# Three queries projected ahead of the first keys, part of the clearing on VectorE, and new stage priorities in a two-layer attention and MLP kernel

## The chip, the cores and the metric

The kernel runs on one core of a Trainium2 chip. The metric is the device time of one execution in microseconds (us). Every kernel below gave the right result. The engines are TensorE (PE in the profile, PEld for its weight loads), VectorE (DVE), ScalarE (ACT), GpSimd (POOL) and SyncE (SP, which here only issues transfers). L803 is line 803 of that kernel's own source, so one operation has different line numbers in different kernels.

## The reference

Two layers of sliding-window attention and MLP over 2048 tokens of 576 elements, in bfloat16; 32 heads of 18 elements, a window of 256.

```
x = x + A(layernorm(x), wqkv, wo)
x = x + B(layernorm(x), w1, b1, w2, b2)
x = x + A(layernorm(x), wqkv, wo)
x = x + B(layernorm(x), w1, b1, w2, b2)

A: q, k, v = x @ wqkv;  s = q k^T / sqrt(18), masked to 0 <= i - j < 256
   softmax(s) @ v @ wo
B: gelu(x @ w1 + b1) @ w2 + b2        # 576 -> 4608 -> 576
```

## The kernel before

The tokens are 16 tiles of 128. They go through each layer in four chunks of four tiles, and the attention of one chunk is laid beside the MLP and the projections of others, so that TensorE always has something to run.

The kernel holds its own list scheduler. Each operation is added with an estimated duration and a priority; the scheduler makes one fixed order for each engine. On the chip each engine then runs its list in that order, and waits where an input is not there.

```python
# the pick: earliest possible start first, then priority
for e in ENGS:
    for t in released[e]:
        st = max(free[e], t.ready)
        ...
        key = (round(st, 3), t.prio, t.idx)
        ...
# emission: the planned order, engine by engine
order = sorted(order + extra, key=lambda x: x[0])
for st, t in order:
    ...
        self.S.add(t.eng, t.fn, names(t.reads), names(t.writes), dma=t.dma, ring=t.ring)
return max(t.end for t in self.tasks)
```

A stage of the program has a name (`q1.0` is the projection of chunk 1, tile 0; `ma`, `mb`, `ga`, `gb` are halves of the MLP; `ea`, `eb` halves of attention; `t` the output projection), and `PL.nudge` adds a number to the priority of all its operations. These numbers were found by annealing. Up to the planned time `FEED_UNTIL` the scheduler also puts back a choice for TensorE that would let ScalarE run dry.

Statistics of a tile, its norm and the casts of queries are on VectorE; the norm is written to one of four buffers `xn`, and SyncE transposes it from there:

```python
add("dve", lambda e, i=i, s=s: e.bn_stats(st_all[:, t, i, :], s[:, t, i * HB:(i + 1) * HB]),
    reads=res, writes=[f"st{t}_{i}"], cost=0.37, lat=0.14, prio=prio)
...
sl = xn_ctr[0] % NXN                                   # NXN = 4
add("dve", lambda e: e.tensor_scalar(xn[:, sl, 0:D], s[:, t, :], mv_all[:, t, 0:1], rstd[:, t:t + 1],
                                      op0=ALU.subtract, op1=ALU.mult),
    reads=res + [f"mv{t}", f"rstd{t}"], writes=[f"xn{sl}"], cost=0.67 if src is None else 0.45, lat=0.14, prio=prio)
...
xin_load(4, 4, ["xa3"], -6)     # input tiles 4 to 7, held back until the first chunk's last transpose
...
xin_load(8, 4, ["k3"], -4)      # input tiles 8 to 11, held back until the fourth key
```

The names in the last two calls are gates only: the loads don't read `xa3` or `k3`, they are held back until these exist. Names in the profiles: `hT` at the start holds the loaded input, `mv_all` and `rstd` its statistics, `xnTa` and `xnTm` are the transposed norms that attention and MLP read, `qn` a cast query, `qT` its transpose, `pT` the exponentials of the scores, `attq` a scaled attention output, `attT` its transpose, `x_res` the residual, and `ps` a bank of PSUM, the memory that matmuls write.

The softmax here doesn't subtract the row's maximum and nothing guards it: scores larger than these inputs give would overflow.

## Time and profile before

| | kernel before |
|---|---|
| time at the outset, 3 runs | 927.13 us (924.19 to 928.40) |
| span of the profiled run | 924.9 us |
| TensorE busy | 900.4 us |
| TensorE idle | 24.5 us |
| VectorE busy | 320.2 us (35%) |
| time lost to TensorE's half clock between 8 and 905 us | 1.71 us, one stretch |

The last row sums 1 minus the granted clock over windows of 1 us (0.36 + 0.50 + 0.50 + 0.35 from 33 to 37 us). The lower clock in the last 0.9 us of the kernel before (0.59, behind its last matmul) is left out.

The prediction shows the busy times, the windows and the timeline. One more view lists what TensorE waited for: the operation that waited, the engine and operation that let it go, us in total, how many times, the longest. The lines of the kernel before with the most time on VectorE, GpSimd and one transfer:

```profile
PE ps L802 <- POOL pT L785: 4.2, 9, 1.0
...
PE ps L669 <- DMA xnTa<-xn: 1.5, 3, 0.8
...
PE ps L669 <- DVE qn L708: 1.1, 4, 0.4
PE ps L919 <- DVE x_res L836: 0.9, 4, 0.3
PE ps L802 <- DVE attq L817: 0.8, 2, 0.5
```

Waits for GpSimd's mask (pT, L785) lead.

A caution: this trace has 9374 matmuls where it has 9411 weight loads. So 37 matmul records are missing, and the idle time is overstated.

### The profile page before, as it was taken

How to read it: one execution, taken by the hardware profiler on the slowest of the kernel's cores; microseconds unless marked ns; L12 is line 12 of the kernel's file. 1: busy time of each engine (PE TensorE's matmuls, PEld its weight loads, DVE VectorE, ACT ScalarE, POOL GpSimd, SP SyncE). 2: the span in 40 equal slices, each digit the busy share in tenths (PEclk: the TensorE clock that was granted, in tenths of full speed). 3: DMA queues.
4: the chain of work that ended last, by engine and by line, in shares of the span. 5: the costliest groups of instructions: out<-in, count | busy, mean ns of one | idle time of the engine just before them, and what ended most of it. 6: DMA issues, size and time to landing. Idle time of an engine off the chain costs nothing.

```text
span 924.9 us, 22416 instructions
## 1 busy us (share of the span) xinstructions
PE 900.4 (97%) x9374; PEld 566.6 (61%) x9411; DVE 320.2 (35%) x796; ACT 598.2 (65%) x721; POOL 373.7 (40%) x507
## 2 busy tenths in 40 slices
PE   9898999999999999999999999999999999999998
PEld 6556475665756657475665657657575665656556
DVE  5647122642217332182324513352111620241001
ACT  4886686676757777566655767557687577852541
POOL 3877453462515535054331644316452363610100
PEclk9999999999999999999999999999999999999999
DMA  8996729743186333944367351693519626174430
GB/s 196 139 242 127 219 57 241 173 145 116 25 211 175 128 105 47 265 98 154 101 99 239 51 188 43 99 264 90 175 40 233 133 69 204 42 202 146 156 116 27
DMA packets 221460, 129.01 MB, mean 139 GB/s; under 512 B 151856, under 2 KB 219184, under 8 KB 221360
## 3 DMA queue, kind: packets, MB, share of 16 engines
q1 hardware_dynamic: 212048, 119.90, 52.3%
q0 software_dynamic: 6880, 5.03, 3.1%
q10 hardware_dynamic: 2432, 2.65, 0.9%
q8 instruction: 74, 1.21, 0.6%
q14 instruction: 26, 0.21, 0.1%
HBM read 91.87 MB, written 2.36 MB: 102 GB/s over the span
## 4 chain that ended last, share of the span: by engine, by line
PE 70%; DMA 3%; issue 2%; DVE 2%; POOL 2%; ACT 1%; POOLq 0%
PE ps L919 25%; PE ps L890 21%; PE ps L669 11%; PE ps L802 6%; PE ps L755 4%; PE ps L878 3%; DMA xnTm<-xn 2%; POOL pT L785 1%; ACT pT L764 1%; DMA xnTa<-xn 1%; DVE xn L613 1%; DVE x_res L836 1%; POOL x_res L901 0%; DVE st_all L590 0%; DVE xn L618 0%
## 5 line engine op out<-in xcount | busy, mean ns | idle before, releaser
L764 ACT ACTIVATE pT<-ps 128x1024 bf16<-128x1024 f32 (+2 forms) x384 | 348.2, 972 | 126.4 <-PE ps L755 125.4
L785 POOL TENSOR_SCALAR_AFFINE_SELECT pT<-pT 128x512 bf16<-128x512 bf16 (+1 forms) x368 | 282.1, 790 | 261.9 <-ACT pT L764 256.2
L919 PE MATMUL ps<-w_sb,hT 128*128 128x288 bf16 x2304 | 314.9, 286 | 1.8 <-DVE x_res L836 0.9
L893 ACT ACTIVATE hT<-ps,b1col 128x512 bf16<-128x512 f32 x288 | 198.0, 687 | 169.3 <-PE ps L890 169.3
L890 PE MATMUL ps<-xnTm,w_sb 128*128 128x512 bf16 x1115 | 255.1, 379 | 3.5 <-issue 2.4
L919 PEld LDWEIGHTS ps<-w_sb,hT 128*128 128x128 bf16 x2304 | 211.4, 97 | 74.0 <-issue 18.5
L890 PEld LDWEIGHTS ps<-xnTm,w_sb 128*128 128x128 bf16 x1152 | 108.9, 98 | 137.5 <-issue 17.4
L836 DVE TENSOR_TENSOR x_res<-ps,x_res 128x288 f32<-128x288 f32 x160 | 71.4, 450 | 257.0 <-PE ps L919 215.0
L669 PE MATMUL ps<-wqkv,xnTa 128*128 128x288 bf16 x960 | 135.8, 288 | 3.9 <-DMA xnTa<-xn 1.5
L802 PEld LDWEIGHTS ps<-vA,pT 128*128 128x128 bf16 x2880 | 94.0, 96 | 28.2 <-POOL pT L785 13.2
L669 PEld LDWEIGHTS ps<-wqkv,xnTa 128*128 128x128 bf16 x960 | 87.0, 98 | 36.4 <-issue 5.8
L802 PE MATMUL ps<-vA,pT 128*128 128x20 bf16 x2880 | 100.2, 171 | 5.3 <-POOL pT L785 4.2
L708 DVE CAST qn<-ps 128x288 bf16<-128x288 f32 x120 | 54.4, 455 | 111.6 <-PE ps L669 108.3
L901 POOL TENSOR_TENSOR x_res<-x_res,b2bc 128x576 f32<-128x576 f32 x32 | 44.9, 1402 | 93.9 <-ACT hT L893 93.9
L755 PE MATMUL ps<-qT,kT 32*128 32x384 bf16 (+2 forms) x1216 | 64.2, 277 | 2.9 <-ACT pT L764 1.9
L601 POOL TENSOR_SCALAR vtmp<-mv_all 128x1 f32<-128x1 f32 (+1 forms) x43 | 8.9, 206 | 131.2 <-DVE mv_all L592 129.8
L695 DVE CAST vA<-ps 128x288 bf16<-128x288 f32 x64 | 29.1, 456 | 54.8 <-PE ps L669 54.7
L590 DVE BATCH_NORM_STATS2 st_all<-x_res 128x6 f32<-128x288 f32 x104 | 44.8, 446 | 3.8 <-DMA x_res<-in_A_x_dram 2.4
L669 PE MATMUL ps<-wo_sb,attT 128*128 128x288 bf16 x320 | 45.0, 286 | 0.2 <-DVE x_res L836 0.2
L812 DVE RECIPROCAL rinv<-ps 128x16 f32<-128x16 f32 x64 | 16.3, 255 | 79.5 <-PE ps L802 79.2
L613 DVE TENSOR_SCALAR xn<-x_res,mv_all,rstd 128x576 bf16<-128x576 f32 x52 | 36.7, 709 | 14.8 <-DMA xnTm<-xn 9.6
L878 PE MATMUL ps<-xnTm,w_sb 64*128 64x512 bf16 x288 | 39.5, 377 | 1.2
(42 smaller groups left out, 279.7 us busy)
## 6 DMA issues: line engine op xcount, KB each, us to landing
w_sb<-in_B_w_dram SPq DMA_DIRECT2D x48, 864.0 KB, 6.3
w_sb<-in_B_w_dram SPq DMA_DIRECT2D x48, 768.0 KB, 4.8
w_sb<-in_B_w_dram SPq DMA_DIRECT2D x96, 48.0 KB, 4.5
x_res<-in_A_x_dram POOLq DMA_DIRECT2D x4, 1152.0 KB, 6.9
out_dram<-xn SPq DMA_DIRECT2D x16, 144.0 KB, 1.8
wqkv<-in_A_wqkv_dram ACTq DMA_DIRECT2D x3, 576.0 KB, 7.5
hT<-in_A_x_dram SPq DMA_DIRECT2D x2, 576.0 KB, 5.0
wo_sb<-in_A_wo_dram ACTq DMA_DIRECT2D x1, 576.0 KB, 6.2
```

The costliest lines, as they stand in the source:

```text
L613: add("dve", lambda e: e.tensor_scalar(xn[:, sl, 0:D], s[:, t, :], mv_all[:, t, 0:1], rstd[:, t:t + 1], op0=ALU.subtract, op1=ALU.mult), r ...
L669: ins = e.matmul(bank(bs[o])[:, 0:HB], lhs(c), rhs(c, o * HB), start=(c == 0), stop=(c == KD - 1))
L708: add("dve", lambda e, b=bs[o], dst=dst: e.tensor_copy(dst, bank(b)[:, 0:HB].rearrange("p (h d) -> p h d", d=DH)), reads=[bs[o]], writes=[ ...
L755: ins = e.matmul(two(bs[j // 2])[:, j % 2, col:col + nq * 128], k_of(T0 + so)[0][32 * j:32 * j + 32, g, :], qs[32 * j:32 * j + 32, g, qo * ...
L764: add("act", lambda e, h2=h2: e.activation(pT[:, sl, 2 * h2:2 * h2 + 2, lo:hi], two(bs[h2])[:, :, lo:hi], ACT.Exp, scale=SCALE), reads=[bs ...
L785: add("pool", lambda e, ap=ap, pat=pat, sgn=sgn, kind=kind: e.affine_select(ap, ap, pattern=pat, compare_op=(ALU.is_ge if kind == "d" else ...
L802: ins = e.matmul(bank(B_O)[:, o:o + VW], pT[:, sl, j, col + qi * 128:col + (qi + 1) * 128], vA[:, (T0 + so) % VS, 4 * g + j, :], start=(fi ...
L836: add("dve", lambda e: e.tensor_tensor(x_res[:, t, sl], bank(b)[:, 0:HB], x_res[:, t, sl], ALU.add), reads=[b], writes=[f"x{t}h{hh}"], cos ...
L878: ins = e.matmul(bank(bk)[:, 0:n], w1_sb[64 * b:64 * b + 64, sl, col:col + 128], xnTm[64 * b:64 * b + 64, k % 2, 4, 0:n], start=True, stop ...
L890: ins = e.matmul(bank(bk)[:, 0:n], w1_sb[:, sl, col:col + 128], xnTm[:, k % 2, c, 0:n], start=False, stop=(c == 3))
L893: add("act", lambda e, ff=ff, fl=fl, bk=bk: e.activation(hT[:, fl, 0:n], bank(bk)[:, 0:n], ACT.Gelu_apprx_tanh, bias=b1col[:, ff:ff + 1]), ...
L919: ins = e.matmul(bank(b)[:, 0:HB], hT[:, fl, i * 128:(i + 1) * 128], w2_sb[:, fl, hh * HB:(hh + 1) * HB], start=(fl == 0), stop=(fl == NFH ...
```

## The change

The intent: the first chunk's queries need a slow transposing transfer (a median 3.3 us to land in the kernel before) and its first keys don't, so three queries go first; GpSimd's clearing at the start is shared with VectorE; the stage priorities are annealed anew for the changed program.

```diff
-FEED_UNTIL = 75.0
+FEED_UNTIL = 40.0
...
-    PL.nudge = {"": 0.63, "ld0+": 7.4, "q1.0": -16.88, "q1.1": 0.39, ...       # 44 numbers, cut
+    PL.nudge = {"": -2.02, "q1.0": -2.58, "q1.1": 0.31, "ln2": 19.43, ...      # 49 numbers, cut
...
-        add("pool", lambda e, i=i: e.memset(qn[:, i, :]..., 0.0), ...)
+        add("dve" if i % 3 == 1 else "pool", lambda e, i=i: e.memset(qn[:, i, :]..., 0.0), ...)
-    add("pool", lambda e: e.memset(attq[:, :, D:KD * 128], 0.0), writes=["aqd"], cost=0.5, prio=-8)
+    add("dve", lambda e: e.memset(attq[:, :, D:KD * 128], 0.0), writes=["aqd"], cost=0.25, prio=-8)
...
-    QK0 = {("q", 0): -5.0, ("k", 0): -4.9, ("q", 1): -4.8, ("q", 2): -4.7, ("k", 1): -4.6, ("q", 3): -4.5, ...}
+    QK0 = {("q", 0): -5.0, ("q", 1): -4.9, ("q", 2): -4.8, ("k", 0): -4.7, ("q", 3): -4.6, ("k", 1): -4.5, ...}
```

## The prediction

> **What bounds the kernel now.** I read the page's busy times first, then windows of 100 us, then the timeline between 24 and 40 us. The busy times:
>
> ```profile
> span 924.9 us, 22416 instructions
> ...
> PE 900.4 (97%) x9374; PEld 566.6 (61%) x9411; DVE 320.2 (35%) x796; ACT 598.2 (65%) x721; POOL 373.7 (40%) x507
> ```
>
> TensorE is busy for 900.4 of 924.9 us, so 24.5 us of it are idle in view. No other engine is above 65%. The list of operations by engine shows that the change removes no matmul of the model: 2304, 1440, 960+320, 2880 and 1408 stay, and only dummy matmuls on the tile `warm` go from 47 to 44. A reordering can therefore win only what lies between matmuls. Where that is:
>
> ```profile
> core 0: us, PE busy (x) PEld busy (x) DVE busy (x) ACT busy (x) POOL busy (x), PEclk, DMA share, GB/s
> 0.00:100.00 100.00, 90.44 (x1189) 61.54 (x1191) 59.90 (x162) 71.55 (x92) 65.33 (x104) 0.98 0.94 170
> 100.00:200.00 100.00, 97.77 (x1064) 59.72 (x1070) 36.21 (x91) 71.59 (x84) 46.15 (x61) 1.00 0.67 163
> ...
> 800.00:925.00 125.00, 120.39 (x889) 74.56 (x892) 23.90 (x58) 52.61 (x69) 16.12 (x22) 1.00 0.43 127
> ```
>
> Idle is 100 - 90.44 = 9.56 us in the first 100 us, 10.3 us in the next 700 (24.5 - 9.56 - 4.61), and 4.6 us at the end. Of that last part 3.35 us follow the last matmul, which ends at 903.75 + 17.80 = 921.55; the order of TensorE after the last attention is the same in both kernels, so it stays. Of the first 9.56 us, 1.11 come before the first dummy and stay too.
>
> The first window also has a mean clock of 0.98. The timeline shows why, and this is the one large flaw that the change can reach:
>
> ```profile
> 28.95 0.79 PE L669 MATMUL ps<-wqkv,xnTa 128*128 128x288 bf16 x5
> 29.57 0.77 PE L802 MATMUL ps<-vA,pT 128*128 128x20 bf16 x24
> 30.88 0.40 PE L755 MATMUL ps<-qT,kT 32*128 32x384 bf16 x8 [0.54 <-DVE mv_all L592]
> 32.07 0.79 PE L669 MATMUL ps<-wqkv,xnTa 128*128 128x288 bf16 x5 [0.79 <-DMA xnTa<-xn]
> ...
> 33.41 1.38 PE L669 MATMUL ps<-wqkv,xnTa 128*128 128x288 bf16 x5
> 34.72 0.51 PE L755 MATMUL ps<-qT,kT 32*128 32x384 bf16 x4
> 35.35 1.38 PE L669 MATMUL ps<-wqkv,xnTa 128*128 128x288 bf16 x5
> ```
>
> At 32.07 the first projection of the second chunk waits for the transposed input. Two idle pieces, 0.54 and 0.79 us, stand together, and from about 33.4 five projections take 1.38 us where they took 0.79. In windows of 1 us the granted clock is 0.64, 0.50, 0.50 and 0.65 from 33 to 37, so 0.36 + 0.50 + 0.50 + 0.35 = 1.7 us of TensorE are lost to the clock. The flaw costs 0.54 + 0.79 + 1.7 = 3.0 us.
>
> Why the input is late is in the transfers:
>
> ```profile
> 24.56 0.37 SPq L534 DMA_DIRECT2D hT<-in_A_x_dram  x1
> 24.73 1.44 DVE L613 TENSOR_SCALAR xn<-hT,mv_all,rstd 128x576 bf16<-128x576 bf16 x4
> ...
> 25.18 6.46 SPq L633 DMA_TRANSPOSE xnTa<-xn  x4
> ...
> 25.63 2.00 POOL L962 DMA_DIRECT2D b1col<-in_B_b_dram  x1
> ```
>
> A load of 576 KB is issued on SyncE just ahead of the four transposes, and GpSimd's bias loads join them. The transposes then take a median 6.2 us to land; those of qT a little earlier took 3.3.
>
> [...] TensorE was 46% and 28% busy in the microseconds from 30 and 31. [...] in the changed program the VectorE clearings of qn have 32x7 elements against 32x14 on GpSimd. [...] no row here shows a clearing that slows GpSimd.
>
> **Part 1, clearing.** GpSimd loses two of six clearings of qn (six take 2.53 us, so 0.42 each) and attq (0.31): 2 x 0.42 + 0.31 = 1.15 us. Its last clearing would end at 4.31 - 1.15 = 3.16 instead of 4.31. But its next work starts at 4.57, after the first tile's statistics (VectorE, 4.27 + 0.21 = 4.48), so none of it is on the path. VectorE gains three. From warm (128 elements, 0.17) and wqkv (864, 0.78) one element costs about 0.83 ns, so 224 elements take 0.25 and 128 take 0.17: 2 x 0.25 + 0.17 = 0.67. It now ends its clearing at 2.22 + 0.30 = 2.52, so then at 3.19; the first tile is picked up at 3.42. Hidden by 0.2 us. Sum: 0.
>
> **Part 2, queries first.** TensorE executes 65 projections before the first scores in the old order and 70 in the new, 5 x 0.122 = 0.6 us more (0.122 us a matmul of 288 columns: the last 144 take 17.80, less a drain of 0.29, over 143). Against that, three queries are ready for their slow transposes about 1 to 2 us earlier, and the key, which needs only TensorE and a copy of 1.01 us, comes later. All of this is filled with projections that have to run anyway, so I count 0 on TensorE. What matters is the issue order on SyncE: in the new one the first transpose of the second chunk's input stands ahead of the 576 KB load, with the other three behind it. The TensorE work before the second chunk's first projection is otherwise the same (120 projections, 36 of the 20-column matmuls, the same scores), plus 3 dummies (0.33 us). I expect the wait at 32.07 to shrink below 0.3 us and the half clock to go: -3.0 + 0.3 = -2.7.
>
> **Part 3, priorities.** Counted as runs of one kind of matmul, the old order has 771 and the new 757. At full rate I get 3584 x 0.1224 + 1152 x 0.216 + 48 groups of edge matmuls x 0.65 + 2880 x 0.026 + some 41 for scores + 8 for transposes and dummies = 843 us. The rest of the busy time, 900.4 - 843 - 1.7 = 56 us, is drain and restart: 56/771 = 0.073 us a run. Fourteen fewer are -1.0 (an estimate from these rows). In the old order two waits for the mask, 0.90 at 81.09 and 0.99 at 84.21, follow long runs of the output projection; in the new one these are spread and 30 more input projections run before the first MLP matmul. I credit half, -0.9. Against this, between the last output projection and the first MLP matmul there now stand 50 input projections, 80 of the small ones and four score groups: 50 x 0.122 + 80 x 0.026 + 4 x 0.3 = 9.4 us, where it was 96.67 - 77.67 = 19.0. In that time the residual, statistics, rstd and norm (about 0.9 + 0.8 + 0.2 + 0.8 + 1.0 = 3.7) and a transpose (3.3 to 6.2) must finish: 7 to 10 us. Two dummies stand just before that MLP matmul, so the scheduler itself left a gap there. I charge +1.0. For the 10.3 us of small idles from 100 to 800, nearly all in pieces under 0.5 us, I expect a net -0.8. Sum: -1.0 - 0.9 + 1.0 - 0.8 = -1.7.
>
> Total: 927.1 - 2.7 - 1.7 = 922.7; I say 922.5.
>
> **Rivals.** (a) The wait moves instead of going. The transposed tile is still caught behind the bias column, whose tiny packets fill the queues (median 9.7 us to land), and the half clock stays: then only part 3, 925 to 927. For it: DMA share is 4.5 and 2.0 in the two microseconds from 30. Against: the tile's transpose now has no large load ahead. (b) The tight path into the first MLP stage becomes a wait of 2 to 3 us that costs the clock a window of 1.7 more: 926 to 929. For it: the arithmetic above and the two dummies. (c) ScalarE is the bound in the first chunk's attention (9.59 of 10 us busy from 60 to 70), so nothing there gets shorter. Against: TensorE holds other work, and its idle in 40 to 80 is only 2.95 us. (d) The new priorities remove half of the idle in 100 to 800 too: 916 to 918.
>
> **Range and chances.** Two per cent is 18.5 us. All idle that this change can touch is 24.5 - 3.35 - 1.11 = 20.0 us with 1.7 for the clock, so faster by 2% would need nearly all of it: 0.02. Slower by 2% would need several clock windows lost and new waits in most stages: 0.01. The old times spread over 4.2 us by themselves. Range 914.5 to 928.5.
>
> **What would show it.** Right: the granted clock is 1.00 from 30 to 40 us, the first 100 us show TensorE busy for about 93, no wait over 0.3 us for xnTa near 32, and the first clearing-dependent work on GpSimd still starts at 4.5. Wrong: a low clock anywhere in 25 to 110 us, a wait of over 1 us for xnTm before the first MLP matmul, or TensorE idle from 100 to 800 us above 13 us or below 6.

## The result, and the profile after

| | before | after |
|---|---|---|
| time, median (lowest to highest), 4 runs each | 926.65 us (924.19 to 928.40) | 934.72 us (934.08 to 935.38) |
| ratio to before, 95% interval | | 1.0089 (1.0064 to 1.0114) |
| span of the profiled run | 924.9 us | 932.9 us |
| TensorE busy / idle | 900.4 / 24.5 us | 900.9 / 32.0 us |
| idle, 100 to 800 us | 10.4 us | 15.2 us |
| lost to half clock | 1.71 us, one stretch | 3.42 us, two stretches |

A ratio is the mean time of one kernel's fast runs over that of the other's in the same rounds, so it isn't quite the ratio of the medians. The change made the kernel 0.9% slower. That is outside my range, and on the other side of the time before.

The page of the kernel after, its span and busy times, and two of its windows of 100 us (columns as in the prediction):

```profile
span 932.9 us, 22409 instructions
...
PE 900.9 (97%) x9372; PEld 566.1 (61%) x9408; DVE 319.9 (34%) x799; ACT 598.4 (64%) x721; POOL 372.0 (40%) x504
```

```profile
0.00:100.00 100.00, 87.98 (x1162) 61.17 (x1163) 64.53 (x167) 67.99 (x88) 61.85 (x98) 0.98 0.92 172
100.00:200.00 100.00, 94.54 (x1017) 56.40 (x1021) 31.19 (x83) 71.66 (x85) 45.02 (x60) 0.98 0.66 157
```

TensorE's busy time grew by 0.5 us only; 7.5 of the 8.0 us are idle time. The first two windows hold most of it: 90.44 - 87.98 = 2.5 us and 97.77 - 94.54 = 3.2 us. The clock of the second window is now below 1 too.

What TensorE waited for in the kernel after, the lines that answer to those of before:

```profile
PE ps L670 <- DVE qn L709: 3.1, 5, 1.5
PE ps L920 <- DVE x_res L837: 3.1, 6, 1.6
PE ps L670 <- DVE x_res L837: 2.5, 2, 1.6
PE ps L803 <- DVE attq L818: 2.5, 3, 1.6
...
PE ps L803 <- POOL pT L786: 2.1, 5, 0.9
```

This is most of the difference in one view. Waits for VectorE are 3.1 + 3.1 + 2.5 + 2.5 and two smaller of 0.6 and 0.5: 12.3 us in place of 4.1. Waits for the mask halved, and those for xnTa are gone. Waits for ScalarE rose too, from 2.7 us to 6.3, with one of 1.89 at 149.85; the last experiment on this kernel, all_moves_3, comes level with the kernel before while they stay at 6.5. Yet VectorE is busy for 34% of the span, as before. So it is not short of time; what TensorE needs from it stands in its queue behind something else. The timeline shows behind what, for the first of the large waits (columns: start, us, engine, line, operation, tiles; in brackets the idle time before it and who ended it):

```profile
26.36 1.42 SPq L535 DMA_DIRECT2D hT<-in_A_x_dram  x1
...
32.20 0.82 DVE L591 BATCH_NORM_STATS2 st_all<-hT 128x6 f32<-128x288 bf16 x2 [1.66 <-DMA hT<-in_A_x_dram]
...
33.22 0.46 DVE L818 TENSOR_TENSOR attq<-ps,rinv 128x288 bf16<-128x288 f32 x1
...
33.82 0.45 PE L803 MATMUL ps<-vA,pT 128*128 128x20 bf16 x12 [1.64 <-DVE attq L818]
```

The load of tiles 8 to 11 goes out at 26.36 us, where it was 24.56: the first transpose now stands ahead of it, as the prediction saw. It lands at about 32.2. In the kernel before it had landed by 29.6, and VectorE's wait for it was short:

```profile
29.56 0.82 DVE L590 BATCH_NORM_STATS2 st_all<-hT 128x6 f32<-128x288 bf16 x2 [0.32 <-DMA hT<-in_A_x_dram]
```

In the kernel after the statistics of tile 8 stand next in VectorE's queue, so VectorE idles 1.66 us for a load nobody needs yet; behind them stands the scaling of an attention output (attq) that frees a PSUM bank, and TensorE waits 1.64 us for it. From 35.7 to 39.1 us its clock is halved.

The second large one, at 180 us:

```profile
180.50 0.80 DVE L614 TENSOR_SCALAR xn<-x_res,mv_all,rstd 128x576 bf16<-128x576 f32 x1 [2.82 <-DMA xnTm<-xn]
181.23 0.44 DVE L837 TENSOR_TENSOR x_res<-ps,x_res 128x288 f32<-128x288 f32 x1
...
181.73 2.35 PE L920 MATMUL ps<-w_sb,hT 128*128 128x288 bf16 x12 [1.63 <-DVE x_res L837]
```

A norm waits 2.82 us for a free `xn` buffer, that is for an earlier transpose out of it; the residual x_res stands behind the norm, and TensorE behind the residual. The four MLP norms of one chunk and four attention norms of another share the four buffers here, and start within 15 us of each other (172.31 to 187.24). In the kernel before all four MLP norms (they start at 172.53 to 181.09 us) come ahead of the first attention norm (183.21). In the kernel after the clock then drops here too:

```profile
183.00:184.00 1.00, 1.00 (x5) 0.36 (x3) 1.00 (x5) 0.00 (x0) 0.61 (x2) 0.50 0.34 65
```

Two more waits of this kind stand at 47.06 (1.46 us, for a cast of a query behind norms) and at 84.02 (1.60 us, for a residual behind a norm). The first of these seems to have a cause on top. VectorE, then GpSimd beside it:

```profile
44.72 2.41 POOL L786 TENSOR_SCALAR_AFFINE_SELECT pT<-pT 128x1024 bf16<-128x1024 bf16 x3
44.78 1.86 DVE L614 TENSOR_SCALAR xn<-hT,mv_all,rstd 128x576 bf16<-128x576 bf16 x2 [0.68 <-POOL rstd L604]
...
46.93 0.76 DVE L614 TENSOR_SCALAR xn<-hT,mv_all,rstd 128x576 bf16<-128x576 bf16 x2
```

Two norms take 1.86 us beside the mask on GpSimd, and the next two, which it overlaps for only 0.2 us, take 0.76. That the mask slows the norms is my estimate from these two rows: no run here moved the mask away to prove it. The scheduler counts 0.45 us for each of these norms.

The trace shows VectorE keeping to its order at 180.50: the residual, whose matmuls had ended by 179.38, starts at 181.23, as the norm that had idled ahead of it ends.

### The profile page after: what moved, and what is told of

Read it like the earlier page. It is cut to its first block, busy times and chain, and to the rows that moved or that the text cites. A ratio compares the mean times of both kernels' runs of the same rounds, so it can differ in the third digit from the quotient of the medians.

```text
span 932.9 us, 22409 instructions
## 1 busy us (share of the span) xinstructions
PE 900.9 (97%) x9372; PEld 566.1 (61%) x9408; DVE 319.9 (34%) x799; ACT 598.4 (64%) x721; POOL 372.0 (40%) x504
## 5 line engine op out<-in xcount | busy, mean ns | idle before, releaser
L591 DVE BATCH_NORM_STATS2 st_all<-x_res 128x6 f32<-128x288 f32 x104 | 44.5, 446 | 12.3 <-DMA x_res<-in_A_x_dram 11.2
L614 DVE TENSOR_SCALAR xn<-x_res,mv_all,rstd 128x576 bf16<-128x576 f32 x52 | 38.2, 737 | 10.6 <-DMA xnTm<-xn 6.9
L756 PEld LDWEIGHTS ps<-qT,kT 32*128 32x128 bf16 x1216 | 19.5, 92 | 34.4 <-issue 21.1
```

The costliest lines, as they stand in the source:

```text
L756: ins = e.matmul(two(bs[j // 2])[:, j % 2, col:col + nq * 128], k_of(T0 + so)[0][32 * j:32 * j + 32, g, :], qs[32 * j:32 * j + 32, g, qo * ...
```

## The experiments

The theory: the slowdown is made of single collisions. At each of them one instruction in a helping engine's queue waits for a transfer or a buffer, what TensorE needs stands behind it, and after some of these stalls TensorE's clock is halved for about 3.4 us, which costs 1.7 us more (after the waits of 1.64 and 1.63 us in the kernel after, not after those of 1.46 and 1.60). Rivals: the new query order or the clearing costs the time by itself; or TensorE's own new order does, so that mending the helpers gives nothing back.

The edits of single places keep the order that the scheduler planned and move named instructions in it before emission, so that TensorE's order and everything else stays. The frame, once:

```diff
+        # planned time, engine, first tile written, new planned time
+        for was, eng, name, new in [...]:
+            hit = [n for n, (st, t) in enumerate(order) if t.eng == eng and abs(st - was) < 0.006 and name in t.writes]
+            order[hit[0]] = (new, order[hit[0]][1])
+        order = sorted(order, key=lambda x: x[0])
+        # and an assertion that all predecessors still stand ahead
```

The results together. Waits are those of TensorE for VectorE (without `warm`), and half-clock stretches those from 8 to 905 us, both from the one profiled run of each kernel; a stretch of double length is counted as two. They vary between runs of one kernel: the mean granted clock of the runs of before lies between 0.998 and 1.000. The kernel before had medians of 926.6 to 926.9; the other kernels have 4 to 6 runs each.

| kernel | median, us | ratio (95%) | waits for VectorE, us | half-clock stretches |
|---|---|---|---|---|
| before | 926.6 | 1 | 4.1 | 1 |
| after | 934.72 | 1.0089 (1.0064 to 1.0114) | 12.3 | 2 |
| load_ahead | 932.57 | 1.0068 (1.0052 to 1.0084) | 7.8 | 2 |
| norm_behind | 936.47 | 1.0107 (1.0090 to 1.0124) | 10.5 | 3 |
| six_moves | 931.53 | 1.0061 (1.0042 to 1.0080) | 4.5 | 1 |
| ring_later | 932.76 | 1.0065 (1.0044 to 1.0087) | 11.2 | 2 |
| all_moves | 929.97 | 1.0030 (1.0008 to 1.0052) | 3.2 | 2 |
| all_moves_3 | 927.91 | 1.0012 (0.9994 to 1.0030) | 4.0 | 1 |
| keys_second_again | 935.38 | 1.0097 (1.0077 to 1.0117) | 10.6 | 3 |
| priorities_alone | 939.84 | 1.0146 (1.0120 to 1.0171) | 11.0 | 3 |
| old_priorities | 933.71 | 1.0069 (1.0047 to 1.0091) | 5.0 | 2 |
| clearing_alone | 927.11 | 1.0001 (0.9977 to 1.0025) | 5.0 | 1 |
| before_load_ahead | 925.15 | 0.9984 (0.9963 to 1.0006) | 5.3 | 0 |
| before_two_edits | 925.06 | 0.9985 (0.9966 to 1.0003) | 2.9 | 0 |

### load_ahead: the kernel after, with one load issued earlier

```diff
+        ld.reads = ()     # the load of tiles 8 to 11: not held back until the fourth key
+        # and placed just ahead of the second chunk's first transpose on SyncE
```

> The changed kernel with its planned order kept on every engine; only the load of input tiles 8 to 11 is issued just ahead of the second chunk's first transpose, and no longer waits for the fourth key. Theory A (late transfers at the head of VectorE's queue): VectorE's wait of 1.66 us for that load at 32.2 us goes, TensorE's wait of 1.64 us at 33.8 goes with it, and the half-clock stretch that follows (3.4 us, worth 1.7) goes too: 3.3 us less than the changed kernel, about 931.4, ratio to before about 1.005. Theory B (the new order itself is worse, waits only move): the time comes back at the next tight place, within 1 us of 934.7.

It came to 932.57 us, 2.1 less than after; the theory wanted 3.3. From the timeline:

```profile
30.27 0.81 DVE L601 BATCH_NORM_STATS2 st_all<-hT 128x6 f32<-128x288 bf16 x2
...
31.93 0.46 PE L813 MATMUL ps<-vA,pT 128*128 128x20 bf16 x12
...
44.02 1.23 PE L680 MATMUL ps<-wqkv,xnTa 128*128 128x288 bf16 x5 [0.96 <-DVE qn L719]
```

The statistics no longer wait for the load, and the matmuls that started at 33.82 after a wait now start at 31.93 without one. But the wait for the cast, at 47.06 in after, is still there (0.96 us), and the half clock now comes with it: the five matmuls of a projection take 1.23 us instead of 0.79. So the cause of the wait at 32 us is shown, and the half clock now follows a later hole. What a hole costs cannot be told from the hole alone: this one of 0.96 us has a half clock behind it (0.61, 0.50, 0.50 and 0.69 from 44 to 48 us), the one of 1.46 us at this place in after had none.

### norm_behind: the kernel after, with the norm at 180 us behind the residual

```diff
+        moves: norm "xn0" 173.22 -> 174.27 and its transpose "xa0" 174.03 -> 174.30
```

> The changed kernel with one instruction of VectorE moved: the normalization of tile 12, which waits 2.82 us at 180.5 us for the transpose that still reads its xn buffer, goes behind the residual and the statistics that stand after it. Theory A: TensorE's wait of 1.63 us at 181.7 and the half-clock stretch from 182 to 186 (1.7 us) both go, 3.3 us less than the changed kernel, about 931.4; the clock stays 1.00 from 100 to 300 us. Theory B: the residual does not hold TensorE, or another wait takes its place: within 1 us of 934.7.

A miss: 936.47 us, no gain. The wait at 181.7 is gone, and another stands 9 us later:

```profile
188.91 0.59 DVE L624 TENSOR_SCALAR xn<-x_res,mv_all,rstd 128x576 bf16<-128x576 f32 x1 [1.86 <-DMA xnTm<-xn]
...
190.30 0.55 PE L813 MATMUL ps<-vA,pT 128*128 128x20 bf16 x16 [1.73 <-DVE attq L828]
```

Another norm of the same eight waits for a buffer, and now an attention output stands behind it. This suggests that the cause is not the place of one norm but that eight norms share four buffers while two sets are mixed; ring_later tests it. This run also had three half-clock stretches where after had two: one at 34 us, and two from 150 to 200 us, where the mean clock is 0.93 and was 0.97 in after.

### six_moves: load_ahead, norm_behind and four other places at once

```diff
+        as load_ahead, and moves: as norm_behind; norm 414.67 -> 416.50 with its transpose; attq 508.82 -> 509.32;
+        two residuals 78.1 and 78.5 -> 76.93; GpSimd's rstd of tiles 8 to 11 40.78 -> 36.06
```

> The changed kernel with both edits above and four more moves of single instructions that stand at the head of a queue while something TensorE needs waits behind them: rstd of tiles 8 to 11 ahead of three masks on GpSimd (TensorE waits 1.46 us at 47.1), two residuals ahead of a normalization (1.60 at 84.0), a normalization behind the casts of the queries (0.59 at 426.7), an attention output behind a residual (0.87 at 521.6). Theory A: 3.3 + 3.3 + 1.46 + 1.6 + 0.6 + 0.9 = 11.2 us if nothing were given back; I expect two thirds, 7 to 8 us, so 926 to 928, equal to the kernel before. Theory B: 932 or more.

931.53 us, 3.2 less than after, where 7 to 8 were expected: a miss that lies between the theory's figure and the rival's. Waits for VectorE are down to 4.5 us. The wait of norm_behind is still there, 1.73 us at 185.72, with the only half-clock stretch right behind it.

### ring_later: the kernel after, with all four attention norms behind the MLP norms

```diff
+        moves: norms of tiles 12 to 15 and their transposes, 173.2 to 179.7 -> 182.8 to 186.6
```

> The changed kernel with its planned order, but the four normalizations of tiles 12 to 15 and their transposes stand 8 to 10 us later, behind the four normalizations of the first MLP's input, as the kernel before has them (the first projection that reads them starts at 204 us in the changed kernel). Theory A, as mended by the two runs above (it is not one instruction: eight normalizations in 12 us share four buffers, each of which is free only when its transpose has landed): VectorE's waits for xnTm of 2.8 us go, the waits of TensorE at 181.7 (1.63) and in the moved form at 190.3 (1.73) stay away, and so does the half-clock stretch: 3.3 us less than the changed kernel, about 931.4. Theory B: another wait takes the place, within 1 us of 934.7.

932.76 us, 2.0 less than after. The wait and the half clock at 181 us are gone, as the theory of the shared buffers has it. In the profiled run the untouched wait at 32 us was longer: it was 1.64 us in after and is 3.33 here, at 35.39 us, with a half clock twice as long behind it (3.4 us lost to it by the windows of 1 us, 1.71 in after). The load took 7.5 us to land where it took 5.8 in after; I did not find why. So this one profile understates what the edit saved at 181, and the size of that saving stays uncertain.

### all_moves: the load, the four norms later, and four single places

```diff
+        as load_ahead and ring_later, and moves: norm 414.67 -> 416.50 with its transpose; attq 508.82 -> 509.32;
+        two residuals 78.1 and 78.5 -> 76.93; GpSimd's rstd of tiles 8 to 11 40.78 -> 36.06
```

> The changed kernel with the load ahead, the four later normalizations and the four single moves of six_moves together. Theory A: six_moves (931.5) less the 3.4 us of the wait and the half clock that it still had between 185 and 192 us: 928 (927 to 929), no half-clock stretch before the end. Theory B: over 931.

929.97 us: 4.75 of some 8.1 us are back, again between the theory's figure (927 to 929) and the rival's (over 931). Waits for VectorE are below those of before. What is left are two half-clock stretches, and waits that are not VectorE's: 1.23 us for a mask at 40.34 us, which I had made myself by putting 1 us of GpSimd's rstd ahead of it, and 1.19 us for a transpose of the attention output at 77.17.

### all_moves_3: two more places

```diff
+        moves: a load of the residual that GpSimd issues 36.13 -> 40.90; a transpose "xa3" on SyncE 67.31 -> 75.05
```

> The changed order with everything of all_moves and two moves more: a load of the residual that GpSimd issues goes behind two masks (in all_moves my own move of the norm's rstd had put 1 us of work ahead of a mask, and TensorE waited 1.23 us for it at 40.3 us and lost the clock), and a transpose whose reader comes 20 us later goes behind the four transposes of the attention output that TensorE waits for (1.19 us at 77.2). Theory (the slowdown is a set of single collisions in the queues of the helping engines, each worth its wait and sometimes a half-clock stretch of 1.7 us): 1.2 + 1.2 + 1.7 for one clock stretch less = 3 to 4 us less than all_moves, about 926 to 927, which is level with the kernel before. Rival (the order is tight as a whole, so each wait that is taken away comes back later): 929.5 to 930.5, and new waits of 1 us or more appear.

927.91 us, ratio 1.0012 with an interval that holds 1. The theory's figure was 926 to 927, the rival's 929.5 to 930.5. TensorE's order is that of the kernel after, instruction by instruction; only the helpers' queues were changed, in one load and 16 moved instructions. With that the kernel is level with before. The median is 0.9 us above the theory's figure, but it decides against the rival that TensorE's order costs the time. One new wait of over 1 us did appear, as the rival had it: 1.13 us for xnTa at 49.81. The last 1 us isn't accounted for; one half-clock stretch is left, at 148 us, behind a wait of 1.9 us for ScalarE that the scheduler's own plan contains. In the profile of after the same wait, 1.89 us at 149.85, has no half clock behind it; what decides this was not shown (see the last section).

### clearing_alone: the kernel before, with the three clearings on VectorE

```diff
+        for st, t in order:
+            if t.tag == "clear":          # two qn buffers and attq
+                t.eng = "dve"             # nothing else is planned anew
```

> The kernel before with its planned order; only the three clearings (two of qn, attq) are issued by VectorE. The prediction says 0: GpSimd's next work still starts at 4.5 us, and VectorE is done with clearing 0.2 us before the first tile is there. A rival: VectorE's clearing reaches past the arrival of the first tile and the start is later by up to 0.5 us. Time within 1 us of before either way; the profile decides: start of the first transpose on TensorE, 7.28 us before.

927.11 us, ratio 1.0001: the clearing is worth nothing, and costs nothing. The first transpose on TensorE, which was to decide, starts at 7.22 us, where it was 7.30.

### keys_second_again: the kernel after, with the old order of queries and keys

```diff
-    QK0 = {("q", 0): -5.0, ("q", 1): -4.9, ("q", 2): -4.8, ("k", 0): -4.7, ...}
+    QK0 = {("q", 0): -5.0, ("k", 0): -4.9, ("q", 1): -4.8, ("q", 2): -4.7, ...}
```

> The changed kernel with the old order of the first chunk's queries and keys, planned anew with the new priorities and the new clearing. If the order of the queries (part 2) is the cause, this is near the time before, 927 to 929. If the cause is in where the new priorities put the later work (part 3), it stays slow: 932 to 936, with waits of over 1 us of TensorE behind VectorE between 100 and 600 us as in the changed kernel.

935.38 us: as slow as after, with 10.6 us of waits for VectorE. With the new priorities the query order isn't what costs the time. The scheduler plans anew here, so this is not an edit of one place.

### priorities_alone and old_priorities: the halves of the change

```diff
 priorities_alone = before, with
+    FEED_UNTIL = 40.0 and the new PL.nudge
 old_priorities = before, with
+    the new QK0 and the three clearings on VectorE
```

> The new stage priorities and the shorter feed in the kernel before: clearing on GpSimd, old order of queries and keys, so the kernel's scheduler plans again (its own plan is 925.7 us against 920.5 for before and 921.2 for after). Theory: a plan drifts on the chip by what it leaves tight, and the new priorities leave more tight spots than the old; drift over the plan 8 to 11 us as in after, so 933.5 to 936.5. Rival 1 (the drift belongs to the one plan, by chance): drift 3 to 6, so 928.5 to 931.5. Rival 2 (the extra time comes with the query order or the clearing): 926 to 928.

> The other half: new query order and clearing on VectorE, the old stage priorities and feed (the kernel's own plan is 926.6 us). Theory: drift over the plan as small as in before, 3 to 6 us, so 929.5 to 932.5, because the old priorities leave the spots looser. Rival (the drift belongs to the one plan): anything up to 11 us, up to 937. If both this and priorities_alone are slower than before, the two parts pay only together, and the 0.7 us by which the plans differ is all that the change was meant to give.

939.84 and 933.71 us, each slower than before, and each above the figure I had given the theory (933.5 to 936.5 and 929.5 to 932.5). For old_priorities the rival, with anything up to 937, covers the result too. A part of that is my own arithmetic: I had counted the drift between plan and chip from aligned instructions in the traces (3.6 us for before, 10.9 for after), and a median lies about 2.5 us further off, for these two kernels. With the medians, the kernels that the scheduler planned itself:

```
kernel              priorities   planned   measured   measured - planned
before              old          920.5     926.6       6.1
old_priorities      old          926.6     933.7       7.1
after               new          921.2     934.7      13.5
keys_second_again   new          921.0     935.4      14.3
priorities_alone    new          925.7     939.8      14.1
```

The planned length is what the kernel's own scheduler returns while the kernel is built. Three things follow. The change was never planned to gain: its plan is 0.7 us longer than that of before. Under the old priorities the new query order and the clearing make the plan itself 6.1 us longer, and most of the 7.1 us that old_priorities loses is there. And the distance between plan and chip goes with the priorities: 6 to 7 us with the old ones, 13.5 to 14.3 with the new ones. Five plans are few, and that the old ones are looser in general is not shown; that these three have more waits for VectorE (10.6 to 12.3 us, against 4.1 and 5.0) is. That these waits are what costs the time was tested for after alone.

### before_load_ahead and before_two_edits: can the kernel before be made faster?

```diff
 before_load_ahead = before, with
+        ld.reads = ()     # tiles 8 to 11 loaded earlier, as in load_ahead
 before_two_edits = before_load_ahead, and
+        moves: two statistics of tile 4, 15.89 and 16.26 -> behind the cast at 16.63; the next cast 18.23 -> 17.485
```

> The kernel before with its planned order; only the load of tiles 8 to 11 is issued as soon as SyncE is free, about 20 us, and not behind the fourth key at 24.6. If the flaw that the prediction named (two waits of 0.54 and 0.79 us at 31 to 32 us and 1.7 us of half clock) comes from that load standing ahead of the transposes, it goes: 3.0 us less than before, about 924, ratio 0.997. If the bias column's packets hold the transposes up by themselves, the wait at 32 us stays: within 1 us of before.

> The kernel before with the early load of tiles 8 to 11 (as in before_load_ahead, 925.15) and with VectorE's statistics of tile 4 behind one cast of a query and the next cast ahead of three other statistics, since in before_load_ahead TensorE waited 1.32 us at 19.5 us for a cast that stood behind statistics whose load had not landed. Theory: that wait goes, 923.7 to 924.3, faster than both kernels. Rival: the statistics come later, so the norms of tiles 4 to 7 and their transposes do too, and the wait moves to the second chunk's first projection: 925 again.

925.15 and 925.06 us, where the theory had about 924 and 923.7 to 924.3. In the first, the two waits at 31 to 32 us and the half clock are gone, which the prediction had valued at 3.0 us; only 1.5 came, and a wait of the same kind grew up at 19 us:

```profile
18.31 0.82 DVE L600 BATCH_NORM_STATS2 st_all<-hT 128x6 f32<-128x288 bf16 x2 [1.87 <-DMA hT<-in_A_x_dram]
19.05 0.44 DVE L718 CAST qn<-ps 128x288 bf16<-128x288 f32 x1
...
19.54 0.48 PEld L679 LDWEIGHTS ps<-wqkv,xnTa 128*128 128x128 bf16 x5 [1.49 <-DVE qn L718]
```

It is the same shape once more: statistics wait 1.87 us for a load, and the cast behind them is what TensorE needs. In the second kernel the cast goes ahead, and the wait becomes one of 0.84 us for the transpose of a query; the median stays at the rival's 925. Both are the fastest kernels here, 1.0% below after with intervals that do not meet. Against before the intervals just reach 1, so it is not shown that they beat it.

## Why the prediction was wrong

The mechanism that I named for each part was mostly there, and the sum had the wrong sign. By its own terms, from the two traces:

| term | predicted, us | found, us |
|---|---|---|
| part 1, clearing | 0 | 0 |
| part 2, the flaw at 31 to 37 us | -2.7 | about +0.7 |
| part 3, fewer changes of kind | -1.0 | -1.2 in busy time, cause not shown |
| part 3, waits for the mask, first 100 us | -0.9 | -1.6 |
| part 3, path into the first MLP | +1.0 | 0 |
| part 3, small idles from 100 to 800 us | -0.8 | +4.7 (3.4 in traces with all records), and +1.7 for the clock |
| not foreseen: casts and residuals at 47 and 84 us | 0 | +3.1 |
| sum | -4.4 | +7.4 of 8.0 |

What is left, 0.6 us (1.9 with the smaller figure), I did not trace.

**Part 2 failed in this step:** "I expect the wait at 32.07 to shrink below 0.3 us and the half clock to go". Its first half was right to the letter: no wait for xnTa is in the list of after, and the projection that started at 32.07 after a wait starts at 30.91. What I left out is who else waits for the load that the transpose overtook. The load landed at 32.2 us, and the statistics that read it stood in VectorE's queue ahead of what TensorE needed. Old: 0.54 + 0.79 + 1.71 = 3.0 us. New: 1.64 + 0.37 behind VectorE + 1.71 = 3.7. load_ahead shows it: with the load earlier, the wait is gone. Rival (a), that the wait moves instead of going, was the right one; the bias column that I named for it was not the cause, since load_ahead still issues it (at 26.02 us, 26.21 in after) and the wait is gone.

**Part 3 failed in "I expect a net -0.8"** for the idle time from 100 to 800 us. It was a guess from the smallness of the pieces, and it left out waits that begin in VectorE's queue. The idle rose from 10.4 to 15.2 us: waits for VectorE by 3.5 us (from 2.0 to 5.5 in that stretch), 1.6 of them at 181 us, and one wait of 1.9 us for ScalarE at 149.85, which the scheduler's plan has too. ring_later shows that the wait at 181 us comes from the mixing of two sets of norms on four buffers. With that and the other places mended, all_moves_3 has 8.9 us of idle time in this stretch, where load_ahead, which leaves them as they were, has 11.5 and clearing_alone 8.1 (all three traces have all records). The waits at 47 and 84 us belong to the same failing: I followed TensorE, ScalarE and SyncE through the new order, and took VectorE at 35% busy for harmless.

**What held.** The clearing: 0, with GpSimd's first dependent work at 4.74 us, where it was 4.57, and no later effect (clearing_alone); in the trace of after VectorE's two clearings of qn (128x224 uint32) take 0.48 us together, and GpSimd's four 1.70, that is 0.42 each as before. Busy time grew by 0.5 us although 1.71 us more went to the clock, so it shrank by 1.2 without it. That fits the 1.0 for fewer changes of kind but doesn't show it: the three dummies fewer are worth about 0.33 of it by the prediction's 0.11 us for one, and in traces with all records busy time less the clock is 899.5 to 902.3 us in six runs of after's order on TensorE and 901.5 to 902.1 in three of before's. The mask waits shrank, by more than I credited (2.5 to 0.9 us in the first 100). The tight path into the first MLP that I charged with 1.0 us, and rival (b), did not come: no wait for xnTm is in the list. Rival (c) was not tested. Rival (d) went the wrong way.

**Its own signs.** It said that a low clock anywhere in 25 to 110 us, or an idle time above 13 us from 100 to 800, would show it wrong. Both came: half clock from 35.7 to 39.1 us, and 15.2 us in a trace that lacks as many records as the one I set the 13 on. TensorE's busy share of the first 100 us, 87.98, was far from the 93 it named.

**The range.** It was built around the sum of expected gains, with the spread of the old times beside it. It had no term for what a new plan does to four other engines' queues. By the table of plans, the distance between plan and chip grew by 1.0 us (old_priorities) to 8.2 (keys_second_again) over that of before, and the plan of keys_second_again is only 0.5 us longer than that of before.

## What to carry to other kernels

Before crediting the removal of a wait, ask for every instruction that the change delays who stands behind it in the same in-order queue; an engine at 35% busy can hold up the bound one when its next instruction waits for a transfer (here VectorE waited 1.66 us for a load at 32.20, and TensorE 1.64 us for what stood behind it). When a change re-plans everything, list TensorE's waits by the engine that ended them, before and after: this one view showed 4.1 us turned into 12.3 where busy times showed nothing. And the length of a plan made of estimated durations did not tell the time on the chip here: plans of 920.5 to 921.2 us ran 926.6 to 935.4. So measure several plans of nearly equal length, and mend the worst collisions by hand.

## What the traces show of the half clock, the norms and the records

- Length and cost: in the kernel after the clock is halved twice, from 35.72 and from 182.50 us (from the share of half clock in the windows of 1 us), for about 3.4 us and at a cost of 1.71 us each; the one stretch of the kernel before costs 1.71 us too. In ring_later and keys_second_again one stretch is twice as long and costs 3.4 us. TensorE was not idle all the time ahead of a stretch: in the kernel after for 1.89 of the 3.42 us ahead of the first and for 1.63 of the 3.41 ahead of the second. The waits of 1.46 us at 47.06 and 1.60 at 84.02 cost no clock.
- One wait for ScalarE of 1.89 us has a half clock behind it in two of these traces and none in two others, with the same matmuls around it. In all_moves (at 149.35) the next four matmuls of 512 columns take 1.66 us, and in ring_later (at 152.11) four take 1.02; in all_moves_3 (at 146.84) the next three in the record take 1.44 us, and in after (at 149.85) the next three take 0.81. So a hole has no fixed price. What decides whether the clock drops was not shown.
- A VectorE norm beside a GpSimd mask: two norms took 1.86 us beside it and two 0.76 us nearly alone. That the mask is the cause was not tested.
- Order in a queue: VectorE, busy for 34% of the span, ended 12.3 us of TensorE's waits, and all_moves_3 brought that to 4.0 by moving instructions, none of them broken up.
- Missing matmul records: 36 or 37 of some 9400 were missing in two traces, and the idle time from 100 to 800 us stood 2.3 and 3.6 us above that of complete traces of the same TensorE order.
